# The first loads on two queues: x rows 2 and 3 issued by ScalarE, wq unbroken on SyncE, q products by token halves

## The chip, the cores and the metric

The kernel runs on one core of a Trainium2 chip, with bfloat16 inputs and output. The metric is device time in microseconds (us). Engines are named as in the profile: PE (TensorE matmul), PEld (its weight loads), DVE (VectorE), ACT (ScalarE), POOL (GpSimd), SP (SyncE, which here only issues DMAs). "SPq" and "ACTq" rows are DMA issues of those two engines.

## The reference

One token batch of 2048 x 512 goes through two branches that a sigmoid gate mixes: an attention with a compressive memory over four segments of 512 tokens (32 heads of 16), and a ReGLU feed-forward with 1792 hidden units.

```
g = sigmoid((x * gate_w).sum(-1, keepdims=True))
q, k, v = x @ wq, x @ wk, x @ wv                 # 32 heads of 16, 4 segments of 512 tokens
for s in range(4):
    p = softmax(qs @ ks.T * 16**-0.5 + mask)     # causal inside the segment
    a_mem = (phi(qs) @ M) / (phi(qs) @ z + 1e-6) # phi(t) = t + 1 if t > 0 else exp(t)
    outs.append(sigmoid(beta) * a_mem + (1 - sigmoid(beta)) * (p @ vs))
    M, z = M + phi(ks).T @ vs, z + phi(ks).sum(0)
a = concat(outs) @ wo
b = (relu(x @ W_gate) * (x @ W_up)) @ W_down
out = g * a + (1 - g) * b
```

## The kernel before, in words

The program is planned in Python while it is built. `program` makes a list of operations (`Op`), each with its engine or engines, what it reads and writes, and an assumed duration; they stand in queues, one for each kind of work, and each queue has one letter. The string `ORDER` (line 24) says which queue gives its next operation, letter by letter; `Sched.place` appends it to its engine's instruction list and adds the semaphore waits that its inputs need. So the order on every engine is written out by hand, as one long string, and `BANKS` (line 37) names the PSUM bank that each accumulation takes. Each engine then runs its own list strictly in order.

PSUM is split in two: `psL`, four banks that hold one block of attention logits at a time, and `psA`, four banks that all other accumulations share. A bank of `psA` can be written again only after DVE or ACT has copied it out.

The work of a segment, as PE sees it:

- L540 / L549 / L547: the products of q, k (channels on the partitions) and v (tokens on the partitions). Segment 0's q products (L540) are made of 256 tokens each, 32 in all: four groups of 128 channels, four rows of wq (`wq0` to `wq3`, 128 input channels each) and two halves of tokens.
- L650: attention logits, one block of 512 columns on four row groups of the array ("quad"), which ACT turns into exponentials (L654, tile `E`) and POOL masks (L659); L682: the products of E with v (`vaug` and a shifted copy `vsh`); L592 and L612: the memory.
- L742: gate and up products of the feed-forward, which ACT or DVE turn into `rl` (L750, L751) and DVE into `hT` (L753); L781 and L774: the down and output products, evacuated at L790 and L791 and stored at L793.

What stands around the change is the start. Segment 0's x is loaded as four row blocks of 128 tokens into `hT` (called x rows 0 to 3 here, 128 KB each), transposed on PE against the identity (L448, 16 products, one for each row block and 128 channels), copied out of psL into `xT` by DVE (L453) and ACT (L455), first for rows 0 and 1 (256 tokens, "half 0"), then for rows 2 and 3 ("half 1"). Five products of constants (L439) and two more (L461) run on PE before there is data. All the loads of the start are issued by SP through `load` (line 355, DMA at L356): x rows 0 and 1, `wq0`, x rows 2 and 3, `wq1` to `wq3`, then wk, wv, half of wg and of wu, two small constants (`braw`, `gwb`), the other halves, and the transposing loads of the next segment's x. Each uses one of 16 semaphores in turn. Three tiny loads of 1 KB (`touch`) are issued by ACT. `gwb` is needed by the gate sums (L491) that DVE makes of the four x rows.

```
    load_x0(0)
    load_x0(1)
    load_w("wq", V.wq, A_wq, (0,))
    load_x0(2)
    load_x0(3)
    load_w("wq", V.wq, A_wq, (1, 2, 3))
```

Of the kernel before, what the change touches and what calls it, by code (L numbers as in the profile page):

```python
# [7 lines left out]
ACT = mybir.ActivationFunctionType  # L8
# [3 lines left out]
F32 = mybir.dt.float32  # L12
# [307 lines left out]
def program(sc, nc, T, PL, PA, A_x, A_wq, A_wk, A_wv, A_wo, A_beta, W_g, W_u, W_d, gate_w, out, NSEG, KT, NF, NT, EPS, SCALE):  # L320
    V = type("V", (), T)

    def op(eng, fn, occ, **k):
        return sc.add(Op([(eng, fn, occ)], **k))

    def pe(fn, occ, **k):
        k.setdefault("lat", PE_LAT)
        if k.get("role") == "w":
            k["reads"] = list(k.get("reads", ())) + [f"init{i}" for i in range(4)]
        return op("pe", fn, occ, **k)  # L330

    def dve(fn, occ, **k):
        return op("dve", fn, occ, **k)
# [4 lines left out]
    def act(fn, occ, **k):  # L338
        return op("act", fn, occ, **k)
# [4 lines left out]
    def dma(eng, fn, nbytes, occ=500.0, **k):  # L344
        return op(eng, fn, occ, dma=True, nbytes=nbytes, **k)

    def A(ep):
        return PA[:, ep.bank, :] if ep.nb == 1 else PA[:, ep.bank:ep.bank + 2, :]

    def xt(c):  # L350
        return [f"xT{c}_{kt}" for kt in range(KT)] if c else [f"xT0_{kt}{h}" for kt in range(KT) for h in range(2)]

    lact, lsp = [], []

    def load(eng, names, dst, src, nbytes, occ=460.0):
        (lact if eng == "act" else lsp).append(dma(eng, lambda e, dst=dst, src=src: e.dma_start(dst, src), nbytes, occ=occ, writes=names, name="ld" + names[0]))  # L356
# [36 lines left out]
    lact = []  # L393
# [42 lines left out]
    def warm(m, n, k, b):  # L436
        def fn(e):
            for i in range(m):
                ins = e.matmul(PL[:, b, 0:n], lhsT=nc.const_aps.tensor(1.0, [128, 128], BF16), rhs=nc.const_aps.tensor(1.0, [128, n], BF16), start=True, stop=True)  # L439
            return ins  # L440
        return pe(fn, m * n * (0.834 if k == 0 else 0.5), writes=[f"bankL{b}"], name=f"warm{k}")

    xps, xcs = [warm(5, 512, 0, 3)], []
    for h in range(2):
        for i in (2 * h, 2 * h + 1):
            for kt in range(KT):
                def fx(e, i=i, kt=kt):
                    return e.matmul(PL[:, kt, 128 * (i % 2):128 * (i % 2) + 128], lhsT=V.hT[:, i, kt * 128:(kt + 1) * 128], rhs=V.ident[:], start=True, stop=True)  # L448
                xps.append(pe(fx, 60 if h else 85, reads=[f"hT{i}", "ident"], writes=[f"bankL{kt}"], name=f"xt{i}_{kt}"))
        for kt in range(KT):  # L450
            src, dst = PL[:, kt, 0:256], V.xT[:, kt, 256 * h:256 * h + 256]
            if kt % 2 == 0:
                xcs.append(dve(lambda e, d=dst, x=src: e.tensor_copy(d, x), t_dve(256), reads=[f"bankL{kt}"], writes=[f"xT0_{kt}{h}"], name=f"xc{kt}{h}"))  # L453
            else:
                xcs.append(act(lambda e, d=dst, x=src: e.activation(d, x, ACT.Copy), t_act(256), reads=[f"bankL{kt}"], writes=[f"xT0_{kt}{h}"], name=f"xc{kt}{h}"))  # L455
# [75 lines left out]
    def proj(s):  # L531
# [3 lines left out]
        def pj(w, col, name, wname, tokmajor=False):  # L535
            ep = epq3 if s == 0 and name == "q" and col == 3 else Epoch()
            if s == 0 and name == "q":
                for k0, h in ((0, 0), (1, 0), (0, 1), (1, 1), (2, 0), (3, 0), (2, 1), (3, 1)):
                    def fh(e, k0=k0, h=h):
                        return e.matmul(A(ep)[:, 256 * h:256 * h + 256], lhsT=w[:, k0, col * 128:(col + 1) * 128], rhs=V.xT[:, k0, tok + 256 * h:tok + 256 * h + 256], start=(k0 == 0 and h == 0), stop=(k0 == KT - 1 and h == 1))  # L540
                    pes.append(pe(fh, mm(256), reads=[f"{wname}{k0}", f"xT0_{k0}{h}"], name=f"{name}{s}_{col}", ep=ep, role="w2" if ep is epq3 or pes and pes[-1].ep is ep else "w"))
                return ep
            for k0 in range(0, KT, 2):
                def fn(e, k0=k0):
                    for kt in range(k0, k0 + 2):
                        if tokmajor:
                            ins = e.matmul(A(ep)[:, :], lhsT=V.xT[:, kt, tok + col * 128:tok + (col + 1) * 128], rhs=w[:, kt, :], start=(kt == 0), stop=(kt == KT - 1))  # L547
                        else:
                            ins = e.matmul(A(ep)[:, :], lhsT=w[:, kt, col * 128:(col + 1) * 128], rhs=V.xT[:, kt, tok:tok + 512], start=(kt == 0), stop=(kt == KT - 1))  # L549
# [343 lines left out]
```

## Time and profile before

| | us |
|---|---|
| median of 3 runs | 265.36 (265.15 to 265.53) |
| the profiled execution | 264.96 |
| its span on the core | 262.9 |
| PE busy | 258.9 |
| ACT busy | 189.5 |
| DVE busy | 183.9 |
| POOL busy | 124.2 |

The span is counted from the first to the last instruction of the program. A timeline row reads: start, duration (us), engine, line, operation, out<-in, number of instructions, and in brackets the idle time of the engine before it with what ended it. Matmul ends are modelled, and successive matmuls overlap: the rate at which PE works is read from the distance of two starts.

### The profile page before, as it was taken

What the parts mean: (1) busy time and instruction counts of PE and PEld (TensorE: products, weight loads), DVE (VectorE), ACT (ScalarE), POOL (GpSimd) and SP (SyncE); (2) the same over time, 40 slices, a digit from 0 to 9 for tenths busy, and PEclk for the clock granted to TensorE, in tenths of its full rate; (3) what the DMA queues carried; (4) which work ended last, traced back from release to release, by engine and by line L of the source; (5) the groups of instructions that cost most, each with busy time, mean ns of one, the idle gap of its engine ahead of it and who ended that gap; (6) DMA issues with size and microseconds to landing.
All of it is one profiled execution on the core that took longest, in us unless ns stands there. A gap on an engine that the chain in (4) does not pass through costs nothing.

```text
span 262.9 us, 6634 instructions
## 1 busy us (share of the span) xinstructions
PE 258.9 (98%) x2761; PEld 115.2 (44%) x2761; DVE 183.9 (70%) x360; ACT 189.5 (72%) x167; POOL 124.2 (47%) x283
## 2 busy tenths in 40 slices
PE   7999999999999999999999999999999999999996
PEld 4644344434344444434434444444444444444444
DVE  5689898878884398887874678967871726569800
ACT  3588898889897787887786797577885767765021
POOL 3038364754546437845454455644653446334000
PEclk9999999999999999999999999999999999999999
DMA  5989535374041222333220230010231000010011
GB/s 178 265 301 268 116 63 144 57 244 86 18 107 42 63 62 41 62 82 60 53 61 16 61 82 22 20 25 3 42 85 37 5 20 22 20 22 0 2 40 42
DMA packets 34686, 19.36 MB, mean 74 GB/s; under 512 B 24033, under 2 KB 34145, under 8 KB 34657
## 3 DMA queue, kind: packets, MB, share of 16 engines
q1 hardware_dynamic: 34560, 18.93, 29.0%
q8 instruction: 22, 0.36, 0.6%
q14 instruction: 8, 0.06, 0.1%
q10 hardware_dynamic: 96, 0.00, 0.0%
HBM read 9.87 MB, written 2.11 MB: 46 GB/s over the span
## 4 chain that ended last, share of the span: by engine, by line
PE 97%; DMA 1%; SPq 1%; issue 0%; DVE 0%
PE psA L742 39%; PE psA L781 19%; PE psA L549 9%; PE psL L650 9%; PE psA L682 7%; PE psA L547 6%; PE psA L774 5%; PE psA L612 1%; PE psA L540 1%; DMA wq<-in_A_wq_dram 1%; SPq L356 1%; PE psA L592 1%; DVE osb L790 0%; PE psL L448 0%
## 5 line engine op out<-in xcount | busy, mean ns | idle before, releaser
L659 POOL TENSOR_SCALAR_AFFINE_SELECT E<-E 64x256 bf16<-64x256 bf16 (+1 forms) x256 | 115.4, 461 | 114.3 <-ACT E L654 106.0
L654 ACT ACTIVATE E<-psL 128x2048 bf16<-128x2048 f32 x72 | 135.1, 1876 | 30.2 <-PE psL L650 28.0
L742 PE MATMUL psA<-xT,wu 128*128 128x512 bf16 x224 | 61.8, 380 | 0.0
L742 PE MATMUL psA<-xT,wg 128*128 128x512 bf16 x224 | 61.0, 380 | 0.0
L781 PE MATMUL psA<-wd,hT 128*128 128x512 bf16 (+2 forms) x238 | 58.2, 367 | 0.0
L753 DVE TENSOR_TENSOR hT<-psA,rl 128x512 bf16<-128x512 f32 x56 | 38.3, 684 | 15.8 <-PE psA L742 14.2
L750 ACT ACTIVATE rl<-psA 128x512 bf16<-128x512 f32 x36 | 21.3, 596 | 16.4 <-PE psA L742 16.4
L781 PEld LDWEIGHTS psA<-wd,hT 128*128 128x128 bf16 x238 | 21.6, 98 | 24.6 <-issue 2.4
L742 PEld LDWEIGHTS psA<-xT,wu 128*128 128x128 bf16 x224 | 20.2, 98 | 25.3 <-issue 3.2
L742 PEld LDWEIGHTS psA<-xT,wg 128*128 128x128 bf16 x224 | 19.9, 98 | 25.2 <-issue 3.9
L650 PE MATMUL psL<-qT,kp 32*128 32x192 bf16 (+7 forms) x512 | 28.8, 287 | 0.1
L692 DVE STREAM_TRANSPOSE Tn<-psA 128x512 f32<-128x512 f32 x32 | 21.1, 695 | 9.0 <-PE psA L682 8.8
L650 PEld LDWEIGHTS psL<-qT,kp 32*128 32x128 bf16 x512 | 8.3, 92 | 26.7 <-issue 11.0
L682 PE MATMUL psA<-E,vaug 64*17 64x128 bf16 (+7 forms) x512 | 18.7, 283 | 0.0
L682 PE MATMUL psA<-E,vsh 64*17 64x128 bf16 (+7 forms) x512 | 18.3, 283 | 0.0
L547 PE MATMUL psA<-wv,xT 128*128 128x512 bf16 x64 | 17.7, 380 | 0.0
L751 DVE TENSOR_SCALAR rl<-psA 128x512 bf16<-128x512 f32 x20 | 13.8, 690 | 4.5 <-PE psA L742 4.2
L790 DVE TENSOR_SCALAR osb<-psA,omg 128x512 bf16<-128x512 f32 (+1 forms) x7 | 4.8, 687 | 17.0 <-PE psA L774 11.0
L549 PE MATMUL psA<-xT,wk 128*128 128x512 bf16 x64 | 16.6, 380 | 0.0
L774 PE MATMUL psA<-wo,oT 128*128 128x512 bf16 (+2 forms) x68 | 16.5, 367 | 0.0
L791 ACT ACTIVATE osb<-psA,omg 128x512 bf16<-128x512 f32 (+1 forms) x10 | 6.8, 676 | 13.0 <-PE psA L774 10.6
L682 PEld LDWEIGHTS psA<-E,vaug 64*17 64x17 bf16 x512 | 11.6, 86 | 7.4 <-issue 3.6
(72 smaller groups left out, 234.7 us busy)
## 6 DMA issues: line engine op xcount, KB each, us to landing
vsh<-vaug SPq DMA_DIRECT2D x8, 272.0 KB, 3.6
out_dram<-osb SPq DMA_DIRECT2D x15, 128.0 KB, 1.7
wg<-in_B_W_gate_dram SPq DMA_DIRECT2D x8, 224.0 KB, 5.6
wu<-in_B_W_up_dram SPq DMA_DIRECT2D x8, 224.0 KB, 5.3
osb<-in_A_x_dram SPq DMA_DIRECT2D x12, 128.0 KB, 2.3
wd<-in_B_W_down_dram SPq DMA_DIRECT2D x3, 512.0 KB, 4.5
hT<-in_A_x_dram SPq DMA_DIRECT2D x4, 128.0 KB, 2.2
wq<-in_A_wq_dram SPq DMA_DIRECT2D x4, 128.0 KB, 2.8
```

The lines of the kernel that those rows point to most:

```text
L547: ins = e.matmul(A(ep)[:, :], lhsT=V.xT[:, kt, tok + col * 128:tok + (col + 1) * 128], rhs=w[:, kt, :], start=(kt == 0), stop=(kt == KT - 1))
L549: ins = e.matmul(A(ep)[:, :], lhsT=w[:, kt, col * 128:(col + 1) * 128], rhs=V.xT[:, kt, tok:tok + 512], start=(kt == 0), stop=(kt == KT - 1))
L650: ins = q.matmul(PL[:, jj, o:o + 512 - 64 * c], lhsT=V.kp[r, kslot(s, G), c, :], rhs=V.qT[r, qslot(s, G), 64 * c:512], start=True, stop=Tr ...
L654: acts.append(act(lambda a: a.activation(V.E[:, e, :, :], PL[:, :, :], ACT.Exp, scale=SCALE), t_act(2048), reads=[f"bankL{b}" for b in ran ...
L659: pools.append(pool(lambda g, ap=ap, base=base: g.affine_select(out=ap, in_=ap, compare_op=ALU.is_ge, fill=0.0, base=base, pattern=[[0, 4] ...
L682: ins = q.matmul(A(eps[p])[32 * jj:32 * jj + 17, 64 * c:512], lhsT=v[:, 8 * G + 2 * jj + p, :], rhs=V.E[r, e, jj, o:o + 512 - 64 * c], sta ...
L692: ds.append(dve(lambda e, p=p, ep=eps[p]: e.transpose(V.Tn[:, p, :], A(ep)[:, :]), 706, writes=[f"Tn{p}"], name=f"tr{s}_{G}_{p}", ep=eps[p ...
L742: ins = e.matmul(A(ep)[:, :], lhsT=w[:, kt, f * 128:(f + 1) * 128], rhs=V.xT[:, kt, c * 512:(c + 1) * 512], start=(kt == 0), stop=(kt == K ...
L750: evs.append(sc.add(Op([("act", lambda e, ep=eg, r=r: e.activation(V.rl[:, r, :], A(ep)[:, :], ACT.Relu), t_act(512)), ("dve", lambda e, e ...
L753: evs.append(dve(lambda e, ep=eu, r=r, hs=hs: e.tensor_tensor(V.hT[:, hs, :], A(ep)[:, :], V.rl[:, r, :], ALU.mult), t_dve(512), reads=[f" ...
L774: ins = e.matmul(A(ep)[:, 0:c1 - c0], lhsT=V.oT[:, o0 + G, i * 128:(i + 1) * 128], rhs=V.wo[:, G, c0:c1], start=st_ and G == 0, stop=sp_ a ...
L781: ins = e.matmul(A(ep)[:, 0:c1 - c0], lhsT=V.hT[:, slots[f], i * 128:(i + 1) * 128], rhs=V.wd[:, f, c0:c1], start=st_ and f == f0, stop=sp ...
```

## The change

x rows 2 and 3 are issued by ACT, behind an exponential of one column that writes a scratch tile, instead of by SP behind `wq0`. SP issues x rows 0 and 1, then all of wq, then goes on as before. Segment 0's q products are put in another order: all four rows of wq with half 0 of the tokens for the four groups (16 products), then group by group the same with half 1 (16 products). The planner is told other sizes for the loads and a due time for the transposes of rows 2 and 3, and the strings `ORDER` and `BANKS` are written anew as a whole, which moves operations on all engines and in all segments.

```diff
 ORDER = (
-    "gefafafefafefafefaefaggfgagggggahgihaisggsagggsggashsigssahsisssasbsssassssassssCassssBsasssCsasBasbasDsasaHEsHasyIaDpasaIwsIasDsaFsysSaIpsFaSwuIauFsa"
...
+    "hafgbgbgfgbgfgbgafgbafgbhhghbhhhhhihbjijbtttbttttbthhhhbthtithjbhttitjtbtttctbttttDbttttCtbtttDtbtCbtbtFtbctIbItFbtbFJqbJtzJJtbEtxbtSvGbttJbHJtSvzbtG"
...
 BANKS = (
-    "012312301230123012301231023012301320312013201320123013201321302310321032031201202012230130120120120130231203120302323013201320132102002302012013013013"
...
+    "012312301230120320321031203213021302130213021302130213012301230123012031031201220203010132302302303210321302013203232013201320312303202030130123123120"
...
-    def load_x0(i):
-        load("sp", [f"hT{i}"], V.hT[:, i, :], x0[:, i, :], 150000)
+    def load_x0(i, eng="sp"):
+        load(eng, [f"hT{i}"], V.hT[:, i, :], x0[:, i, :], 140000)
...
-            load("sp", [f"{nm}{kt}"], w[:, kt, :], src[kt * 128:(kt + 1) * 128, :], 410000 if (nm, kt) == ("wk", 0) else 160000)
+            load("sp", [f"{nm}{kt}"], w[:, kt, :], src[kt * 128:(kt + 1) * 128, :], 360000 if (nm, kt) == ("wk", 0) else 140000)
     load_x0(0)
     load_x0(1)
-    load_w("wq", V.wq, A_wq, (0,))
-    load_x0(2)
-    load_x0(3)
-    load_w("wq", V.wq, A_wq, (1, 2, 3))
+    load_w("wq", V.wq, A_wq, range(KT))
+    lact.append(act(lambda e: e.activation(V.rden[:, 0:1], nc.const_aps.tensor(1.0, [128, 1], F32), ACT.Exp), 1500, writes=["rden"], name="tab"))
+    load_x0(2, "act")
+    load_x0(3, "act")
+    sc.queue(0, lact)
     load_w("wk", V.wk, A_wk, range(KT))
...
+                if h:
+                    xps[-1].after = 5400.0
...
-                for k0, h in ((0, 0), (1, 0), (0, 1), (1, 1), (2, 0), (3, 0), (2, 1), (3, 1)):
+                for k0, h in ((0, 0), (1, 0), (2, 0), (3, 0), (0, 1), (1, 1), (2, 1), (3, 1)):
```

The sizes given to `load` and the time `after` only steer the planner's bookkeeping; the data moved is the same.

The order at the start of PE before (L439 and L461 are the products of constants, L448 the transposes of x, L540 the q products, L549 the k products):

```order
1 L439 MATMUL psL<-const-bfloat16-1.0 128x512 x5
2 L448 MATMUL psL<-ident,hT 128x128 x8
3 L461 MATMUL psA<-const-bfloat16-1.0 128x256 x2
4 L540 MATMUL psA<-xT,wq 128x256
5 L448 MATMUL psL<-ident,hT 128x128 x2
6 L540 MATMUL psA<-xT,wq 128x256
7 L448 MATMUL psL<-ident,hT 128x128 x3
8 L540 MATMUL psA<-xT,wq 128x256
9 L448 MATMUL psL<-ident,hT 128x128 x2
10 L540 MATMUL psA<-xT,wq 128x256 x2
11 L448 MATMUL psL<-ident,hT 128x128
12 L540 MATMUL psA<-xT,wq 128x256 x27
```

And of the change (lines are three further down; L653 is a block of logits, L550 the v products, L745 the gate and up products):

```order
4 L543 MATMUL psA<-xT,wq 128x256 x8
5 L449 MATMUL psL<-ident,hT 128x128 x5
6 L543 MATMUL psA<-xT,wq 128x256
7 L449 MATMUL psL<-ident,hT 128x128
8 L543 MATMUL psA<-xT,wq 128x256 x2
9 L449 MATMUL psL<-ident,hT 128x128 x2
10 L543 MATMUL psA<-xT,wq 128x256 x21
11 L552 MATMUL psA<-xT,wk 128x512 x14
12 L653 MATMUL psL<-qT,kp 128x512 x4
13 L552 MATMUL psA<-xT,wk 128x512 x2
14 L550 MATMUL psA<-wv,xT 128x512 x6
15 L745 MATMUL psA<-xT,wg 128x512 x2
```

Eight q products now stand ahead of the first transpose of x row 2, where one stood; the fifth transpose of the half is the first that needs x row 3. The last row of wq is first needed by the 13th q product, and 20 q products remain from there.

ACT at the start of the change, whose first rows before were the table load, the four copies into xT and the first tiny load:

```order
1 L369 ACT_TABLE_LOAD
2 L369 ACTIVATE rden<-const-float32-1.0 128x1
3 L356 DMA hT<-in_A_x_dram 128x512 x2
4 L458 ACTIVATE xT<-psL 128x256 x4
5 L356 DMA adT<-in_B_W_gate_dram 16x32
```

The table load belongs to the new exponential; the two x loads follow it.

DVE of the change, from the copy of k's last group to the first gate sums (L494, which need gwb) and the `hT` product after them:

```order
6 L565 CAST kT<-psA 128x512
7 L531 TENSOR_SCALAR ttmp<-kT 128x1024
8 L578 CAST vaug<-psA 128x32x16
9 L569 TENSOR_SCALAR kp<-kT,pm 128x8x64 x2
10 L532 TENSOR_TENSOR ek<-ek,ttmp 128x1024
11 L578 CAST vaug<-psA 128x32x16
12 L754 TENSOR_SCALAR rl<-psA 128x512
13 L531 TENSOR_SCALAR ttmp<-kT 128x1024
14 L756 TENSOR_TENSOR hT<-psA,rl 128x512
15 L494 ISA hT,gl<-hT,gwb 128x512
...
17 L494 ISA hT,gl<-hT,gwb 128x512
...
19 L756 TENSOR_TENSOR hT<-psA,rl 128x512
```

Before, all four v copies of this segment, the small constants made from `braw` and the first `hT` product stood ahead of the first gate sum; now two v copies and that `hT` product do, and the second `hT` product, which frees the bank of the second up accumulation, waits behind two gate sums.

More of the change, by code (lines that the diff above doesn't have):

```diff
@@ new lines @@
+    "eTAvTtJtMeDTqtTJxvETvTvAvMzTqdArMTvxAvprQMUUyAqTtUAtxTtATdtUGtTtHATqSvHvAxVRtMTtTvAvVHqRtLATvxdTtJvCTtTtJtFMTqTtoxvdvCTptTMtTqTSFrxSvATVvvAzTvMqTVtTLA"
+    "vTRxttAdCvvAtMTqFvToxtvMTptTtJtDJvATFqTvMxTvTtMrozqTpAvTWxvAvWMttAHtTAvHAvLqTAsTxvPTouuMunTnpPqTuoxPTuTuXuuTqOuTJxYJupTsuTPuPuPTqTuXTxsTuPtPuPtTOXqTGu"
+    "xYsuPuPuyTPqTupTxRuXvrSTSyquATxvTAuTvMTvuNKTTAKYvTRvuALRvqMTvxvovMpurMTqVTQvxAuvSrVAUUMTquUAxTuATuUtBvoquxATpvSvtMTVvTHNqTvxTMVvTvJvJMTvYTqovxvMTpvTve"
+    "MTvTAvLvMeTqTArxeMTvAvevTALqTvAxTvTMvvAvoLvAvnMTnpqTLvAxvosTMtTtPvBDvPTAqTLvpTPxvTvBtMvtTLtETtrKJCqRWtxAvWAttEtTqADtTAxvAvtMTtTEtTqADTtTxtBvETXvtMtTqH"
@@ L36 @@
+    "wwwwwOwwwwwYNY"
 )
 BANKS = (
-    "012312301230123012301231023012301320312013201320123013201321302310321032031201202012230130120120120130231203120302323013201320132102002302012013013013"
-    "21020230232013201320132013201320201313210310210210210231023102312312312320"
+    "012312301230120320321031203213021302130213021302130213012301230123012031031201220203010132302302303210321302013203232013201320312303202030130123123120"
+    "32020230120123012301230213021301312012032321020201201201230120312031203120"
```

16 lines of the change are left out of this document (6 added, 10 removed).

## The prediction

> **What bounds the kernel now.** I read the page first (the span and PE's share), then the chain of waits, then the list of waits with PE alone, then the timeline of PE and of SP over the first 10 us.
>
> ```profile
> span 262.9 us, 6634 instructions
> PE 258.9 (98%) x2761; PEld 115.2 (44%) x2761; DVE 183.9 (70%) x360; ACT 189.5 (72%) x167; POOL 124.2 (47%) x283
> PE psL L439 <- PEq L878: 0.8, 1, 0.8
> PE psA L540 <- DMA wq<-in_A_wq_dram: 0.5, 1, 0.5
> PE psA L540 <- DVE xT L453: 0.2, 1, 0.2
> ```
>
> The last three rows are the whole list of PE's waits: who waited for whom, total, times, longest. PE waits for the program's start, and twice during the first q products; after those it never waits again in 250 us. So PE's own work sets the end, and an edit can move it in three ways only: PE starts its unbroken run earlier, its run gets longer, or a wait appears in it.
>
> The work in the run is the same after the change. The two orders hold the same products, and PE goes over between the full array (q, k, v, feed-forward, output) and the tiled products (logits, E with v, memory) 164 times in both, so that the price of going over cancels too. The last rows are also alike: the same wo and wd products of the last three token blocks in the same order. What is left is the start and new waits.
>
> The start on PE:
>
> ```profile
> 2.93 1.06 PE L448 MATMUL psL<-ident,hT 128*128 128x128 bf16 x8
> 4.50 0.27 PE L540 MATMUL psA<-xT,wq 128*128 128x256 bf16 x1 [0.20 <-DVE xT L453]
> 5.00 0.33 PE L448 MATMUL psL<-ident,hT 128*128 128x128 bf16 x3
> 6.14 0.28 PE L540 MATMUL psA<-xT,wq 128*128 128x256 bf16 x1 [0.49 <-DMA wq<-in_A_wq_dram]
> 6.26 0.22 PE L448 MATMUL psL<-ident,hT 128*128 128x128 bf16 x1
> 6.32 3.11 PE L540 MATMUL psA<-xT,wq 128*128 128x256 bf16 x27
> 9.27 3.19 PE L549 MATMUL psA<-xT,wk 128*128 128x512 bf16 x14
> ```
>
> Between the first q product at 4.50 and the first k product at 9.27 lie 32 q products and eight transposes. A q product takes (3.11 - 0.27) / 26 = 0.109 us from start to start, a transpose (0.33 - 0.22) / 2 = 0.055. That is 3.49 + 0.44 = 3.93 us of work in 4.77; the other 0.84 is lost, most of it before `wq1` landed. I call the start of the k products T; it is 9.27 now, and from there 253 us of work follow without a wait.
>
> **The change part by part.** I work T out as the latest of four bounds.
>
> PE's own work: the first q product still waits for `wq0` and the first copy, so T cannot be below 4.50 + 3.93 = **8.43**.
>
> The loads on SP:
>
> ```profile
> 2.19 0.91 SPq L356 DMA_DIRECT2D hT<-in_A_x_dram  x2
> 3.14 1.38 SPq L356 DMA_DIRECT2D wq<-in_A_wq_dram  x3
> 3.14 2.96 DMA wq<-in_A_wq_dram
> wq<-in_A_wq_dram SPq DMA_DIRECT2D x1, 128.0 KB, 2.8
> hT<-in_A_x_dram SPq DMA_DIRECT2D x1, 128.0 KB, 2.4
> 4.56 1.85 SPq L356 DMA_DIRECT2D wk<-in_A_wk_dram  x4
> wk<-in_A_wk_dram SPq DMA_DIRECT2D x1, 128.0 KB, 3.2
> ```
>
> The third row is from the chain: `wq1` is issued at 3.14 and lands 2.96 later, at 6.10; PE goes on at 6.14. The rows with one DMA and a last number are its time from issue to landing, for `wq3` (issued at 3.14 + 1.38 - 0.43 = 4.09, landed at 6.89), for x row 3 (2.67, 5.07) and for `wk3` (5.98, 9.2). SP issues every (1.38 - 0.43) / 2 = 0.475 us.
>
> `wq3` now stands where `wq1` stood, sixth on SP, and is issued at 3.14. Its landing lies between 6.10, if ACT's two loads take nothing from it, and 6.89, if the eight loads of x and wq land no faster together than the eight before. The DMA engines' share decides between the two:
>
> ```profile
> 3.00:4.00 1.00, 1.00 (x11) 0.93 (x9) 0.45 (x3) 0.19 (x1) 0.05 (x1) 1.00 0.80 241
> 5.00:6.00 1.00, 0.66 (x9) 0.42 (x6) 0.64 (x2) 0.38 (x1) 0.00 (x0) 1.00 0.84 226
> 8.00:9.00 1.00, 1.00 (x12) 0.90 (x10) 0.41 (x1) 0.60 (x1) 0.00 (x0) 1.00 0.98 303
> ```
>
> (The last two columns are the busy share and GB/s.) At 3 to 6 us they were 80 to 84% busy, with 226 to 241 GB/s; at 8 us 98% and 303. So a second issuer finds room for about a fifth more, and I take 6.4, nearer to the lower end. From `wq3` on, 20 q products remain, 4 of half 0 and 16 of half 1: T = landing + 0.04 + 20 x 0.109 = landing + 2.22, which is **8.62** (8.32 to 9.11).
>
> A rule of the Trainium skill speaks against this step: "DMA: Bandwidth & Descriptors", section "Issuing engines are not separate DMA queues", says that DMAs from several engines share the same 16 DMA engines, and that issuing from more than one saves only the issuing time. The busy share of 0.80 in the row above agrees that there was issuing time to save, and the 0.98 that there is little more; taken strictly the rule gives the upper end, and that case is the first rival below.
>
> x row 3 on ACT:
>
> ```profile
> 0.80 1.28 ACT L455 ACT_TABLE_LOAD   x1 [0.80 <-PEq L878]
> 6.52 0.38 ACT L455 ACTIVATE xT<-psL 128x256 bf16<-128x256 f32 x1 [0.61 <-PE psL L448]
> 6.53 0.38 ACTq L356 DMA_DIRECT2D adT<-in_B_W_gate_dram  x1
> 3.71 0.76 DVE L453 CAST xT<-psL 128x256 bf16<-128x256 f32 x2 [0.55 <-PE psL L448]
> adT<-in_B_W_gate_dram ACTq DMA_DIRECT2D x1, 1.0 KB, 3.0
> adT<-in_B_W_up_dram ACTq DMA_DIRECT2D x1, 1.0 KB, 3.8
> adT<-in_B_W_down_dram ACTq DMA_DIRECT2D x1, 1.0 KB, 5.9
> ```
>
> ACT's DMA of 6.53 is issued as soon as the activation ahead of it has begun, so the two x loads leave when the exponential begins, at 0.80 + 1.28 = 2.08, and about 0.43 later, at 2.5: 0.1 to 0.2 before SP issued them. If ACT lets them pass the waiting exponential they leave at 0.8 and 1.2 and land earlier; x rows 0 and 1 then share the DMA engines with them, which moves 4.50 rather than the end of the list. With the 2.4 of x row 3 the landing is at 4.9, with the 3.0 of ACT's first load at 5.5. After it come 0.04, four transposes (0.22), 0.26 from a transpose to its copy (6.26 to 6.52), two copies (0.76) and 14 products (1.53): T = landing + 2.81, so 7.7 to 8.3. It does not bind. The exponential costs nothing: ACT had the table load at that time anyway and nothing to do until 3.81.
>
> wk: SP issues it two places, 0.95 us, earlier. The second pair of k products needs `wk3` at T + 0.43; at the worst it lands at 9.2 as now, which gives T = 8.81, with its latency kept at 8.25 and T = 7.9. Below the 8.62 for all but the worst part.
>
> Sum: T = 8.62 instead of 9.27, **0.65 us less**, bounds 0.16 and 0.84.
>
> New waits in the rewritten order can take some of it back. The densest place that I find is the DVE list of the first segment, where two gate sums, which need gwb, now stand ahead of the second `hT` product:
>
> ```profile
> 12.73 0.43 SPq L356 DMA_DIRECT2D gwb<-in_gate_w_dram  x1
> gwb<-in_gate_w_dram SPq DMA_DIRECT2D x1, 128.0 KB, 6.3
> L753 DVE TENSOR_TENSOR hT<-psA,rl 128x512 bf16<-128x512 f32 x5 | 3.4, 688 | 0.7 <-ACT rl L750 0.5 <-PE psA L742 0.2
> L529 DVE TENSOR_TENSOR ek<-ek,ttmp 128x1024 bf16<-128x1024 bf16 x2 | 1.7, 826 | 0.0
> L566 DVE TENSOR_SCALAR kp<-kT,pm 128x512 bf16<-128x512 bf16 x8 | 2.8, 367 | 0.2
> L528 DVE TENSOR_SCALAR ttmp<-kT 128x1024 bf16<-128x1024 bf16 x2 | 1.3, 642 | 0.0
> 20.59 1.18 DVE L491 CUSTOM_DVE_ANT_0 hT<-hT,gwb 128x512 bf16<-128x512 bf16 x1
> 22.51 0.68 DVE L753 TENSOR_TENSOR hT<-psA,rl 128x512 bf16<-128x512 f32 x1
> 13.36 0.69 DVE L562 CAST kT<-psA 128x512 bf16<-128x512 f32 x1
> 18.00 0.40 PE L650 MATMUL psL<-qT,kp 32*128 32x256 bf16 x8
> 18.33 0.60 PE L547 MATMUL psA<-wv,xT 128*128 128x512 bf16 x2
> ```
>
> DVE copies k's last group at T + 4.09 (13.36 now). With that copy, ten steps lead to the first gate sum: five of 0.69 (copies, relu, `hT`), two of 0.64, two of 0.37, one of 0.83, in all 6.3 us, so T + 10.4, which is 19.0. gwb lands at 12.73 + 6.3 = 19.0 now, and not later after the change. Two gate sums take 22.51 - 20.59 = 1.92, `hT` 0.69: the bank is free at T + 13.0. PE asks for it (by `BANKS`) with the fourth gate accumulation, after 56 products of (3.19 - 0.38) / 13 = 0.216 and three blocks of logits that each add 0.33 + 0.1: T + 13.4. It is covered with 0.4 to spare; if gwb came at 19.4 the cover would be gone, and each later us costs PE one. For the rest of the order I take no wait, since the list above shows none in 250 us of the order before; the bounds of that are 0 and, if one such place in each segment fell short by its 0.4, 1.6.
>
> The profiled execution took 264.96, 2.06 more than its span, and 0.40 less than the median of 265.36. 264.96 - 0.65 = 264.31 on its scale, **264.7** as a median.
>
> **The rivals.** *The transfers were the bound all along.* All eight loads land as before, `wq3` at 6.89, T = 9.11: 265.2, no change. For it: landings already trailed issues by more and more (2.4 for x row 3, 2.8 for `wq3`, 3.2 for `wk3`). Against it: the busy share of 0.80. *Slower: x row 3 comes late from ACT's queue*, and PE stands before its transposes with eight q products done and all else behind them. ACT's own small loads took 3.0, 3.8 and 5.9. It decides from a landing at 9.27 - 2.81 = 6.46 on, a latency of 4.0; with 5.9 it lands at 8.4, T = 11.2, and the median is 267.3; with 4.6 at 7.1, 266.0. Against it: the 5.9 was met at 15.9 us with the DMA engines full. *The new order gives it back*: the gate sums meet a gwb at 19.9, or another bank is short, 0.5 us in all: 265.2. *The change does not do what it says*: ACT issues the x loads only after the exponential has ended and its queue has started up, say 0.4 later, 5.9 for x row 3, T = 8.7: 264.8, hardly told from the forecast.
>
> **How the numbers follow.** About 0.2% of the median, 0.53 us, is what a measurement of this kernel can tell from no change. The forecast has 0.50, the transfers as the bound 0.25, the late x row 0.10, the new waits 0.15. Faster by over 0.53 needs a median below 264.83, T below 8.74 without new waits: most of the first case, 0.45. Slower takes the late x row and the worse part of the new waits: 0.19. The rest, 0.36, lies within. The range reaches from 264.3 (T at its lowest, 264.5, and a measurement's 0.2) to 266.0.
>
> **What would show it.** T, the first k product's start, at 8.4 to 8.8 and PE's waits below 0.5 us between the first q product and T; a landing of `wq3` near 6.4 and of x row 3 before 5.8; no PE wait after T. I am wrong if T is above 9.0, or if the list of PE's waits has new rows after T that sum to more than 0.3 us.

## The result, and the profile after

The change makes the kernel slower: 265.86 us median of 22 runs against 264.93 us median of 22 runs of the kernel before on the same chip, ratio 1.0053 with a 95% interval of 1.0033 to 1.0073 (the ratio is of means without one run of 331.03; the medians alone give 1.0035). The forecast was 264.7. The runs of the change stand in two groups: 13 at 265.26 to 266.05 and 8 at 267.14 to 268.51; those of the kernel before make one group, 264.01 to 265.93. The profiled run of the change took 267.23 and belongs to the upper group; its span is 265.3, 2.4 more than before.

The page, and the whole list of PE's waits:

```profile
span 265.3 us, 6637 instructions
PE 260.9 (98%) x2761; PEld 116.1 (44%) x2761; DVE 186.6 (70%) x364; ACT 185.9 (70%) x164; POOL 123.1 (46%) x283
PE psL L440 <- PEq L881: 0.8, 1, 0.8
PE psL L653 <- issue: 0.7, 1, 0.7
PE psA L543 <- DMA wq<-in_A_wq_dram: 0.3, 1, 0.3
```

PE sets the end as before, with as many products and 2.0 us more of busy time: it worked more slowly somewhere. One wait is new, and no engine and no DMA is named as its releaser: "issue".

The timeline of ACT, SP and PE at the start:

```profile
0.80 1.28 ACT L369 ACT_TABLE_LOAD   x1 [0.80 <-PEq L881]
0.86 0.87 ACTq L356 DMA_DIRECT2D hT<-in_A_x_dram  x2
2.10 0.20 ACT L369 ACTIVATE rden<-const-float32-1.0 128x1 f32<-128x1 f32 x1
1.73 3.40 DMA wq<-in_A_wq_dram
3.19 1.30 PE L449 MATMUL psL<-ident,hT 128*128 128x128 bf16 x8
5.27 1.86 PE L543 MATMUL psA<-xT,wq 128*128 128x256 bf16 x8 [0.34 <-DMA wq<-in_A_wq_dram]
6.93 0.74 PE L449 MATMUL psL<-ident,hT 128*128 128x128 bf16 x5
8.42 2.76 PE L543 MATMUL psA<-xT,wq 128*128 128x256 bf16 x21
11.01 1.24 PE L552 MATMUL psA<-xT,wk 128*128 128x512 bf16 x5
```

Three things are to be seen. ACT issues its two x loads at 0.86, while the table load runs and before the exponential at 2.10: they pass it. They then share the DMA engines with x rows 0 and 1 and `wq0`, which lands at 1.73 + 3.40 = 5.13 instead of 4.37, and the first q product starts at 5.27 instead of 4.50. And the eight q products from 5.27 to 6.93 are (6.93 - 5.27) / 8 = 0.21 us apart, twice the 0.109 of the kernel before. T is 11.01, not 8.62.

The new wait, in PE's timeline:

```profile
46.37 0.66 PE L595 MATMUL psA<-vaug,phik 128*32 128x34 bf16 x64
46.96 1.04 PE L745 MATMUL psA<-xT,wg 128*128 128x512 bf16 x4
49.03 0.39 PE L653 MATMUL psL<-qT,kp 32*128 32x256 bf16 x6
50.09 0.28 PE L653 MATMUL psL<-qT,kp 32*128 32x256 bf16 x2 [0.67 <-issue]
```

It falls inside a block of logits, after six of its eight products. The program places its waits for semaphores only ahead of a block, so no semaphore can be the cause: the last two starts at the wait are 0.94 us apart. The kernel before has the same break, unnoticed because the list of waits doesn't show it, inside its block at 47.16, where two starts are 0.40 apart (that block takes 0.80 instead of 0.40):

```profile
44.23 1.90 PE L547 MATMUL psA<-wv,xT 128*128 128x512 bf16 x8
47.16 0.80 PE L650 MATMUL psL<-qT,kp 32*128 32x256 bf16 x8
```

The 2.42 us by which PE ends later in the profiled run are then T with 1.74, this break with 0.54, and 0.13 at the third block of logits (22.5 us), which waits for an exponential that ACT began 1.2 us late. ACT was late because each of its three 1 KB loads into `adT` waits until the one before has landed; they now start at 8.67 instead of 6.53 and meet full DMA engines, and the exponential of 20.53 stands behind the third:

```profile
8.67 0.34 ACTq L356 DMA_DIRECT2D adT<-in_B_W_gate_dram  x1
13.31 0.37 ACTq L356 DMA_DIRECT2D adT<-in_B_W_up_dram  x1
20.17 0.32 ACTq L356 DMA_DIRECT2D adT<-in_B_W_down_dram  x1
20.53 1.88 ACT L657 ACTIVATE E<-psL 128x2048 bf16<-128x2048 f32 x1 [1.58 <-PE psA L745]
```

### The profile page after: what moved, and what is told of

It is laid out like the page before. It is cut to its first block, busy times and chain, and to the rows that moved or that the text cites. A ratio compares the mean times of both kernels' runs of the same rounds, so it can differ in the third digit from the quotient of the medians.

```text
span 265.3 us, 6637 instructions
## 1 busy us (share of the span) xinstructions
PE 260.9 (98%) x2761; PEld 116.1 (44%) x2761; DVE 186.6 (70%) x364; ACT 185.9 (70%) x164; POOL 123.1 (46%) x283
## 4 chain that ended last, share of the span: by engine, by line
PE 92%; DMA 6%; ACT 1%; issue 0%; SPq 0%; DVE 0%; ACTq 0%
PE psA L745 36%; PE psA L784 19%; PE psL L653 9%; PE psA L552 8%; PE psA L685 7%; PE psA L777 5%; PE psA L550 4%; DMA adT<-in_B_W_up_dram 3%; DMA adT<-in_B_W_gate_dram 2%; DMA wq<-in_A_wq_dram 1%; PE psA L615 1%; PE psA L543 1%; ACT E L657 1%; PE psA L595 1%; PE psL L449 0%
## 5 line engine op out<-in xcount | busy, mean ns | idle before, releaser
L745 PE MATMUL psA<-xT,wg 128*128 128x512 bf16 x224 | 60.9, 380 | 0.0
L745 PE MATMUL psA<-xT,wu 128*128 128x512 bf16 x224 | 60.5, 380 | 0.0
L784 PE MATMUL psA<-wd,hT 128*128 128x512 bf16 (+2 forms) x238 | 57.1, 367 | 0.0
L784 PEld LDWEIGHTS psA<-wd,hT 128*128 128x128 bf16 x238 | 20.9, 98 | 24.2 <-issue 4.3
L745 PEld LDWEIGHTS psA<-xT,wu 128*128 128x128 bf16 x224 | 20.2, 98 | 25.6 <-issue 2.8
L745 PEld LDWEIGHTS psA<-xT,wg 128*128 128x128 bf16 x224 | 20.4, 98 | 25.2 <-issue 2.4
L653 PE MATMUL psL<-qT,kp 32*128 32x192 bf16 (+7 forms) x512 | 28.8, 287 | 0.7 <-issue 0.7
L754 DVE TENSOR_SCALAR rl<-psA 128x512 bf16<-128x512 f32 x28 | 19.2, 687 | 10.3 <-PE psA L745 10.1
L753 ACT ACTIVATE rl<-psA 128x512 bf16<-128x512 f32 x28 | 16.7, 596 | 12.2 <-PE psA L745 12.2
L653 PEld LDWEIGHTS psL<-qT,kp 32*128 32x128 bf16 x512 | 8.3, 92 | 26.6 <-issue 11.5
L552 PE MATMUL psA<-xT,wk 128*128 128x512 bf16 x64 | 17.3, 380 | 0.0
L550 PE MATMUL psA<-wv,xT 128*128 128x512 bf16 x64 | 16.9, 379 | 0.0
L793 DVE TENSOR_SCALAR osb<-psA,omg 128x512 bf16<-128x512 f32 (+1 forms) x10 | 7.1, 706 | 12.7 <-PE psA L777 11.7
L794 ACT ACTIVATE osb<-psA,omg 128x512 bf16<-128x512 f32 (+1 forms) x7 | 4.7, 671 | 14.6 <-PE psA L777 14.0
```

Of the source, the lines that this page charges most:

```text
L653: ins = q.matmul(PL[:, jj, o:o + 512 - 64 * c], lhsT=V.kp[r, kslot(s, G), c, :], rhs=V.qT[r, qslot(s, G), 64 * c:512], start=True, stop=Tr ...
L745: ins = e.matmul(A(ep)[:, :], lhsT=w[:, kt, f * 128:(f + 1) * 128], rhs=V.xT[:, kt, c * 512:(c + 1) * 512], start=(kt == 0), stop=(kt == K ...
L754: ("dve", lambda e, ep=eg, r=r: e.tensor_scalar(V.rl[:, r, :], A(ep)[:, :], 0.0, None, ALU.max), t_dve(512))],
L784: ins = e.matmul(A(ep)[:, 0:c1 - c0], lhsT=V.hT[:, slots[f], i * 128:(i + 1) * 128], rhs=V.wd[:, f, c0:c1], start=st_ and f == f0, stop=sp ...
```

## The experiments

The theories, as they stood after the two traces. **Clock**: PE starts at half rate and reaches its full one only after some time of work without a break; the later x row 1 and `wq0` make breaks. **Order**: the rewritten lists bring their own waits, whatever the loads do; later this became **fetch**: PE's instructions come by DMA in pieces, and PE runs out of them. **Transfers**: the loads alone decide. Each comparison is with runs of the kernel before on the same chip in the same batch; the ratio compares means, the first two columns are medians.

| run | median us | before | ratio, 95% interval | runs above 266 |
|---|---|---|---|---|
| e1 start filled | 266.09 | 264.74 | 1.0034 to 1.0079 | 7 of 11 |
| e2 loads put back | 266.67 | 264.74 | 1.0049 to 1.0095 | 9 of 11 |
| e3 loads held | 265.73 | 264.74 | 1.0026 to 1.0070 | 3 of 12 |
| e4 loads alone | 264.70 | 264.74 | 0.9985 to 1.0027 | 3 of 12 |
| e5 list shifted 37 | 264.64 | 264.65 | 0.9993 to 1.0032 | 2 of 12 |
| e6 before, shifted 35 | 264.87 | 264.65 | 1.0000 to 1.0033 | 1 of 12 |
| e7 shifted 65 | 265.57 | 264.65 | 1.0018 to 1.0047 | 2 of 12 |
| e8 three repairs | 264.37 | 264.65 | 0.9975 to 0.9996 | 0 of 12 |
| e9 shifted 80 | 265.82 | 265.08 | 1.0013 to 1.0043 | 3 of 12 |
| e10 shift, 1 KB loads freed | 264.54 | 265.08 | 0.9983 to 1.0031 | 4 of 12 |
| e11 shift, start filled | 264.90 | 265.08 | 0.9980 to 1.0005 | 0 of 12 |
| e12 repairs, old order | 265.04 | 265.08 | 0.9985 to 1.0022 | 2 of 12 |
| e13 wd behind | 265.44 | 264.85 | 1.0009 to 1.0054 | 5 of 12 |
| e14 before, wd ahead | 267.53 | 264.85 | 1.0077 to 1.0126 | 6 of 6 |
| e15 wo and wd behind | 265.08 | 264.85 | 1.0007 to 1.0054 | 5 of 12 |
| e16 the change again | 266.10 | 264.85 | 1.0034 to 1.0077 | 7 of 12 |

**Loads or order?** e1 to e4 take the change apart.

e1 gives PE work in the breaks:

```diff
+    def warm_m(e):   # placed behind the transposes of x row 0
+        for _ in range(2):
+            ins = e.matmul(PL[:, 3, 256:512], lhsT=<ones 128x128>, rhs=<ones 128x256>, start=True, stop=True)
...
     def warm1(e):
-        for _ in range(2):
+        for _ in range(4):
```

> The change with PE's idle time at the start filled: two more products of constants (128x256) between the transposes of x row 0 and those of x row 1, and four instead of two ahead of the first q product. Clock theory (PE works at half rate until it has been busy without a break for some us, and the breaks that the later x row 1 and wq0 make put this off in some runs): no run above 266.5, q products 0.109 us apart soon after the first one, T 9.2 to 9.5, time 265.3 to 265.8. Rival (the slow q products have nothing to do with PE's breaks): 3 to 4 runs in 10 stay at 267 to 268.5 as with the change.

e2 has the loads of before with the order of the change:

```diff
-    load_w("wq", V.wq, A_wq, range(KT))
+    load_w("wq", V.wq, A_wq, (0,))
+    load_x0(2)
+    load_x0(3)
+    load_w("wq", V.wq, A_wq, (1, 2, 3))
...
-    load_x0(2, "act")
-    load_x0(3, "act")
```

> The change with its loads put back: x rows 2 and 3 on SP behind wq0, the exponential kept, the new order of all operations kept. Clock theory: first q product at 4.5, T about 9.1 (wq3 at 6.9 + 2.2), one group of times and none above 266.5. Order theory (the rewritten order costs 0.135 us at the fourth block of logits and 0.54 us near 50 us whatever the loads do): both waits are still there, time 265.2 to 265.6. If all of the loss came from the loads: 264.5 to 264.9.

e3 makes ACT's loads wait for the exponential's result:

```diff
     def load_x0(i, eng="sp"):
-        load(eng, [f"hT{i}"], V.hT[:, i, :], x0[:, i, :], 140000)
+        load(eng, [f"hT{i}"], V.hT[:, i, :], x0[:, i, :], 140000, reads=["rden"] if eng == "act" else ())
```

> The change with ACT's two x loads made to wait for the result of the exponential, so that they leave at about 2.4 and 2.8 as the prediction assumed. Clock theory and the prediction's sum: x rows 0 and 1 land at 2.85 and 3.23, wq0 at 4.4, the first q product starts at 4.5, q products 0.109 apart, T 8.5 to 8.9, no run above 266.5; time 264.4 if the new order costs nothing, 264.9 to 265.2 if its two waits (0.135 and 0.54) remain. Rival (wq3 is bound by the transfers whichever engine issues): T 9.1, 265.4 with the waits.

e4 is the kernel before with the lines of the change on the loads (the exponential, x rows 2 and 3 on ACT, all of wq on SP) and its own order otherwise:

> The kernel before with the loads of the change alone (exponential and x rows 2 and 3 on ACT, wq unbroken on SP), its own order of everything else. Clock theory: the first q product starts near 5.3, T is 9.2 to 9.4 in most runs and about 11 in 3 to 4 runs in 10, so times of 264.9 to 265.2 and 266.5 to 267. Order theory: the waits at 22.5 and 50.1 us are absent. If the loads are harmless: one group, 264.5 to 265.

e4 against the others answers it: the loads alone cost nothing in the median (264.70 against 264.74; three of 12 runs are above 266, where the 33 of the kernel before have none), while all three kernels with the new order lose 1.0 to 1.9 us, e2 with the loads of before among them. e1 and e2 missed: neither has a single group, and e2 should have come out at 265.6 at most. Their profiles say why. The break that I had taken for a fixed 0.54 isn't fixed:

```profile
PE psL L660 <- issue: 2.5, 1, 2.5
PE psL L654 <- issue: 1.7, 1, 1.7
PE psL L653 <- issue: 1.3, 1, 1.3
```

These are PE's waits inside the same block of logits in e1, e2 and e3. Against the 0.40 of before, the distance of the two starts grew to 2.75, 1.95 and 1.56.

On the loads e3 shows the rest. With the hold, x rows 0 and 1 and `wq0` land at 2.83, 3.23 and 3.95, and the first q product starts at 4.21; but q products stay 0.21 apart, and transposes 0.107, until 6.35, so T is 9.24 (worked out from the last q product, since that trace lacks the first k product). e2 is alike, at half rate until 6.6.

**Instructions as data.** The page counts the DMAs that bring instructions:

```profile
q8 instruction: 22, 0.36, 0.6%
```

They are 16 KB each. PE's list has 2761 products, each with its weight load, and some 50 separate waits, about 5570 instructions. 0.36 MB over these is 64 bytes each, so q8 fits PE's list, and a piece holds 256 instructions; in e5, whose list stands 37 products later, the third of these DMAs starts at 40.36 instead of 47.77. Counted in the traces, the break stands in both kernels ahead of the same place, about the 960th instruction, though other work stands there. In every profile that has the break, PE goes on 2.3 to 2.9 us after the third of these DMAs has started (before: 45.36 to 47.67; the change: 47.77 to 50.09; e1: 47.42 to 50.02). Fitted over the complete traces, a DMA mostly starts some 1 to 3 us after PE has come within about 300 instructions of the border. Ahead of this border those 150 products are 64 products of the memory (0.66 us), 64 of E with v (1.1 us), two blocks of logits and a few large ones, 4.3 us in all before and 4.4 in the change; every other border of the two has 7.9 us or more.

e5 moves the border off that stretch, by small products of constants in place of the large ones at the start, for as long:

```diff
-    xps, xcs = [warm(5, 512, 0, 3)], []
+    xps, xcs = [warm(42, 64, 0, 3)], []
```

> The change with the five products of constants at the start (128x512) replaced by 42 small ones (128x64) that should fill the same 2.3 us. Nothing else differs, but each product stands 37 places later in PE's list of instructions. Fetch theory (PE runs out of fetched instructions at the 467th product, because the 121 products before it, small ones of the memory and of E with v, take only 2.7 us, less than a fetch needs): by the profile of the change the shortest such stretch is then 5.0 us, so the wait inside the block of logits near 50 us is gone and no other takes its place; most runs at 264.5 to 265.0, some above 266 left from the half rate of the start. Rival (the wait belongs to that place in the program: a semaphore, a bank, E with v): it is still there, 265.5.

e6 does it in the kernel before (`warm(40, 68, 0, 3)`), e7 and e9 shift the change further, to where I reckoned another dense stretch (60 of 128x45 and 12 of 128x44 for `warm1`; 70 of 128x39 and 17 of 128x30):

> The kernel before with 40 small products of constants (128x68) in place of its five large ones, so that its list stands 35 places later. Fetch theory: the stretch of 121 products that took 3.8 us and cost a wait of 0.37 at 47.7 us gives way to a shortest one of 5.1; the wait goes and the time falls by 0.3 to 0.5, to 264.2 to 264.5. Rival: no difference, 264.7.

> The change with its list put 65 places later instead of 37 (60 products of 128x45 at the start and 12 of 128x44 in place of the later two). Fetch theory: the wait near 50 us is gone here too, but a stretch of 121 products that takes only 1.6 us (from 161.0 to 162.7 in the profile of the change) now stands just where a fetch is due, so PE waits 1.5 to 4 us in a block of logits near 162.7 us; time 266.5 to 269. Rival (shifting the list only removes a wait at one place, or does nothing): 264.6 to 265.5.

> The change with its list put 80 places later (70 products of 128x39 at the start, 17 of 128x30 in place of the later two). Fetch theory with exact counts: PE's waits so far came each time ahead of the 962nd instruction of its list (two for a product, one for a separate wait) in the kernels of both orders, and a new piece of 256 instructions begins every 256 from there; the shift by 65 put such a border behind a stretch of 140 products that took 5.1 us, which was enough; the shift by 80 puts it behind one that takes 2.5 us (160.5 to 163.0 in the profile of the change). So PE waits 1 to 3 us for an issue between 162 and 164 us, the wait near 50 us is gone, and the time is 265.8 to 268. Rival (fetches are late only early in the program, or with other loads running): no wait there, 264.5 to 265.5.

e5 is the clean hit: 264.64 against 264.65 for the kernel before, where the unshifted change is 0.93 to 1.25 above it, and nothing differs after the start but 37 places in the list. No PE wait over 0.2 is left after T in its profile (the 0.2s there are single products that the trace lacks), the one at the third block neither. In e6 the break is gone too, but the time did not fall as expected; its profile shows another stretch that broke:

```profile
20.04 0.23 ACT L468 ACTIVATE eb<-braw 128x32 f32<-128x32 bf16 x1 [2.38 <-DMA braw<-in_A_beta_dram]
PE psL L650 <- ACT E L654: 1.1, 1, 1.1
```

`braw` landed at 20.0 instead of 17.35, ACT stood before it, and PE behind ACT. e7 and e9 missed: no wait came at 162 us. In e9 the DMA had started at 157.8 with 287 instructions to go, 3.5 us ahead of the border: the stretch before it was longer than I had counted, since I let the DMA be due 280 instructions ahead and it is due earlier, at about 300; with that it is 4.7 us. In e9's profile PE waits 1.0 us for the late `eb` constant at 28 us instead. What else costs e7 and e9 their 0.7 to 0.9 isn't settled.

**The sum without the losses.** e8 is e3 and e5 together, with the 1 KB loads under names of their own, so that none waits for another:

```diff
     def touch(n, src):
-        load("act", ["adT"], V.adT[0:16, 32 * n:32 * n + 32], src, 1024)
+        load("act", [f"tch{n}"], V.adT[0:16, 32 * n:32 * n + 32], src, 1024)
```

> The change with three repairs: ACT's two x loads wait for the exponential, the list is shifted by 37 places with 42 small products, and the three 1 KB loads on ACT no longer wait for one another. Theory (loads, fetch and those waits together were the whole loss): first q product at 4.2 to 4.5, no PE wait after T over 0.2, T between 8.5 and 9.5 depending on when PE comes to its full rate; 263.9 to 264.6, below before. Rival (half rate at the start takes all that the loads could win, whatever is repaired): 264.6 to 265.2.

e10 is e5 with the freed 1 KB loads, e11 is e5 with the filled start of e1, e12 is the kernel before with e8's three repairs:

> The run with the list shifted by 37 places, with the three 1 KB loads on ACT freed from one another and nothing else. If those waits cost (0.135 us at the fourth block of logits in the profile of the change), the median is 264.4 to 264.6; if they are covered, as with the shift alone, 264.6 to 264.7. The x loads still pass the exponential, so 1 to 3 runs in 12 above 266 remain, and the distance from here to the run with all three repairs (264.37, none above 264.9) is what the real wait for the exponential brings.

> The shift by 37 places and the filled start together (38 products of 128x70, two of 128x256 between x rows 0 and 1, four ahead of the first q product). Clock theory (the runs above 266 of the shift alone come from breaks in PE's work, which put off its full rate): none above 265.8, median 264.5 to 264.9. Rival (those runs have another cause): 1 to 3 of 12 above 266.

> The kernel before, its own order of everything but the start's loads, with the three repairs of the fastest run so far: x rows 2 and 3 on ACT behind a real wait, the list 35 places later (no stretch of 140 products under 7 us at a border), the 1 KB loads freed. If the rewritten order itself is worth nothing once fetches are out of the way: 264.2 to 264.5, as there. If the new order of the q products is worth something: 264.6 to 265.0. If this order keeps the late small constant that cost 1.1 us in the shifted kernel before: a group at 265.5.

e8 is faster than the kernel before, 264.37 against 264.65, the interval just below 1, all runs within 263.87 to 264.86. Its start:

```profile
4.30 0.61 PE L543 MATMUL psA<-xT,wq 128*128 128x256 bf16 x4
5.34 0.61 PE L543 MATMUL psA<-xT,wq 128*128 128x256 bf16 x4 [0.43 <-DMA wq<-in_A_wq_dram]
6.71 2.46 PE L543 MATMUL psA<-xT,wq 128*128 128x256 bf16 x21
```

The products are 0.109 apart from the start, and T is 6.71 + 21 x 0.1095 = 9.01: even here `wq1`, landed at 5.29, holds PE for 0.43 after four products, and x row 3, landed at 6.10, once more. e10 against e5 tells nothing of the 1 KB loads, since its runs again stand in two groups, 264.25 to 264.57 and five from 265.71 on. That grouping is the test of the clock theory, with the break out of the way: with ACT's loads let pass and the start unfilled 2 of 12 (e5) and 4 of 12 (e10) are above 266; with the start filled (e11) or the loads held (e8) none of 24 is. That is 6 of 24 against none; that half rate is behind those six is argued from the one profile of the upper group, the change's at 267.23, since no run above 266 of e5 or e10 was profiled. In e12, two of whose runs are above 266, held loads did harm: its order wants x row 2 after the first q product, it landed at 6.12, and PE stood for 1.4 us.

```profile
6.17 0.29 PE L449 MATMUL psL<-ident,hT 128*128 128x128 bf16 x2 [1.41 <-DMA hT<-in_A_x_dram]
```

**Why the fetch is later in the change.** Both orders have the dense stretch; the change loses more there. SP's list differs: the change puts the first 512 KB load of wd ahead of two transposing loads, right behind wo and an x row.

```profile
42.22 0.58 SPq L356 DMA_DIRECT2D wo<-in_A_wo_dram  x1
42.84 0.51 SPq L499 DMA_DIRECT2D osb<-in_A_x_dram  x1
43.39 0.43 SPq L356 DMA_DIRECT2D wd<-in_B_W_down_dram  x1
45.00:46.00 1.00, 1.00 (x6) 0.29 (x3) 1.00 (x4) 1.00 (x2) 0.16 (x1) 1.00 1.07 376
46.00:47.00 1.00, 1.00 (x74) 0.72 (x74) 1.00 (x3) 1.00 (x2) 0.66 (x2) 1.00 1.08 384
45.00:46.00 1.00, 1.00 (x6) 0.29 (x3) 1.00 (x2) 1.00 (x1) 0.85 (x2) 1.00 0.39 127
```

The first two windows are of the change; their last columns, share and GB/s, show full DMA engines until 47 us. The last row is the kernel before, where the share falls to 0.39 at 45 to 46, when its fetch starts. e13 moves wd back behind the two transposing loads, e15 moves wo too, e14 moves wd ahead in the kernel before; only letters of SP's queue in `ORDER` change places. e16 is the change itself.

> The change with one DMA moved in SP's list: the first 512 KB load of wd, which the new order puts ahead of two transposing loads of ek, goes back behind them, where the kernel before has it. PE's list isn't shifted. Theory (PE's fetch of instructions, due near 45 us, stands behind the 512 KB loads of wo and wd on the DMA engines; with both in front of it, it starts at 46.2 to 47.8 and PE waits 0.9 to 2.7): the fetch starts earlier, the wait in the block of logits near 50 us falls to 0.5 or less, median 264.9 to 265.3. Rival (the dense run of small products alone makes the fetch late, whatever is loaded): the wait stays at 0.9 to 2.7, time as with the change.

> The kernel before with the same DMA moved the other way: the first load of wd right behind wo and the x row, ahead of the two transposing loads. Theory: the fetch of 45.4 us comes 0.5 to 2 us later and the wait of 0.4 us at 47.3 grows to 0.9 to 2.5; median 0.4 to 1.5 above before, with nothing else changed. Rival: no difference beyond 0.2.

> The change with both large loads, wo and the first of wd, behind the two transposing loads. Theory: the DMA engines are free when the fetch is due, it starts 0.9 to 1.5 us after PE passes the 304th instruction ahead of the border, as at the other borders, and PE waits less than 0.2; median 264.5 to 264.9, as with the shifted list, with the few runs above 266 that the start makes. Rival: as the change.

> The change itself, once more beside the others on the same chip. Theory: q products at half rate for between 1 and 4 us after the first one, T between 9.2 and 11, a PE wait of 0.5 to 2.7 near 50 us whose end stands 2.3 to 2.6 after the start of a fetch; median 265.5 to 266.2.

e14 is the sharpest run of the study: one DMA moved ahead makes the kernel before 2.7 us slower. Its profile, PE first and then windows of one us:

```profile
46.73 0.39 PE L650 MATMUL psL<-qT,kp 32*128 32x256 bf16 x5
48.78 0.29 PE L650 MATMUL psL<-qT,kp 32*128 32x256 bf16 x3 [1.66 <-issue]
47.00:48.00 1.00, 0.11 (x5) 0.00 (x0) 1.00 (x2) 0.27 (x1) 1.00 (x4) 1.00 0.00 0
49.00:50.00 1.00, 1.00 (x8) 0.51 (x6) 0.00 (x0) 0.89 (x1) 0.00 (x0) 0.95 0.53 106
50.00:51.00 1.00, 1.00 (x4) 0.30 (x2) 0.00 (x0) 0.98 (x1) 0.00 (x0) 0.50 0.39 59
51.00:52.00 1.00, 1.00 (x4) 0.34 (x3) 0.22 (x1) 0.00 (x0) 0.88 (x3) 0.50 0.92 264
52.00:53.00 1.00, 1.00 (x4) 0.42 (x3) 1.00 (x3) 0.00 (x0) 0.71 (x2) 0.50 0.69 242
```

The fetch started at 46.30, 0.9 later than before though PE came to the border 0.4 sooner, and the wait grew to 1.66. What follows is a second loss: the granted clock (third column from the right) falls to 0.50 for 3.4 us, which costs some 1.6 us more. Its mean over the run, 0.994, marks such runs: four of e14's six have it, and elsewhere it stands only at the slowest runs of kernels with the break (268.51 of the change, 268.79 of e1, 268.47 and 269.94 of e2, 268.75 of e3, 268.29 of e16). No run of a shifted kernel has it. Nor does each break bring it: after the longer wait of 2.5 in e1's profile the granted clock stays at 1.00.

e13 met the expected break, 0.3 us at most in its profile (264.63 us), but not the median: five of its runs are above 266, which fits the unfilled start, though none of the five was profiled. e15 missed: with both loads gone the DMA engines moved nothing from 43 to 45 us, and yet the fetch started 2.3 us after it was due, not 0.9 to 1.5, and PE waited:

```profile
43.00:44.00 1.00, 1.00 (x6) 0.29 (x3) 1.00 (x4) 1.00 (x2) 0.17 (x1) 1.00 0.00 0
44.00:45.00 1.00, 1.00 (x74) 0.74 (x74) 1.00 (x3) 1.00 (x2) 0.65 (x2) 1.00 0.00 0
PE psL L653 <- issue: 0.5, 1, 0.5
```

So the dense stretch alone cost up to 0.72 by the distance of the two starts, and with both large loads in front of the fetch it was 0.94 to 2.75. What sets the 1 to 3 us from due to start, 2.3 in e15 with the DMA engines idle, stays open. e16 shows the break at 1.4 us and T at 9.71 with products at full rate, waiting 1.0 us for `wq0`.

## Why the prediction was wrong

*What bounds the kernel* was right: PE's busy time sets the end, no step of ACT, DVE or POOL took its place. But "an edit can move it in three ways only" left out a fourth: PE's own rate. And the list of waits, from which I read that PE "never waits again in 250 us", hid a wait of 0.4 in the kernel before that sat inside a busy group.

*PE's own work, T not below 8.43.* This step failed. It priced 32 q products at 0.109 and eight transposes at 0.055, and held that 4.50 would stay. The rate held in the kernel before because its PE waited for `wq1` until 6.14 anyway, so that any half rate up to there cost nothing; once wq comes unbroken, the rate is what T hangs on. Measured: first q product at 5.27, products 0.21 apart to 9.05, T = 11.01 in one run, 9.71 at full rate in another. A page of the Trainium skill has the rule, and the prediction left it out: "TensorE: Matmul & The Clock Gate", section "Part 1: The HAM clock gate", says that PE works at half its clock until it has been busy for a window of about 3.4 us that runs free of the kernel's start, so that the point varies from run to run. By it, as an estimate, an unbroken start at 0.84 would come to full rate between 4.2 and 7.6; the traces agree (at or before 4.8 in the kernel before, 6.35 in e3, 6.6 in e2), and the one profile of the upper group, with breaks in its start, has it at 9.05. Breaks don't always put it off: e16's start has longer ones, and its first q products, from 5.77, are 0.109 apart.

*x row 3 on ACT, "the two x loads leave when the exponential begins".* Wrong, and the sentence behind it had the truth: they left at 0.86 and 1.28 and moved the first q product from 4.50 to 5.27. The prediction named this and then gave it neither a place in the sum nor a rival. The row of 6.53 was read too widely: the activation ahead of that DMA waited for PE, and the exponential waits for nothing. That x row 3 doesn't bind came true by luck: it landed at 4.43 because it left early. Held as the prediction assumed, it landed at 5.84 in e3 and at 6.10 in e8, after the 4.9 to 5.5 expected; with the prediction's own 2.81 that gives T = 8.65 and 8.91, above its 8.62.

*The loads on SP.* `wq3` at 6.4 was nearly right: 6.55, between the two bounds (6.78 in e3 and 6.47 in e8, where the x loads leave as assumed). What SP's later loads gained, the first ones lost: x row 1 came 0.6 and `wq0` 0.8 later. e4 puts the sum of it at zero, as the rival of the transfers had it, for another reason.

*New waits.* The DVE place did hold, and gwb landed at 18.77. "For the rest of the order I take no wait" failed twice: 0.13 on ACT's chain of 1 KB loads, and the fetch with 0.54 in one profile, 1.3 in the other and up to 2.35 in kernels that share the order. The upper bound given, 1.6, was of the right size, but its mechanism was a bank; the rival that the new order gives it back had 0.15 and should have led. e5 shows that this term carries the loss of the lower group: without it the median is that of the kernel before.

*The sum* of 0.65 less was not met by any version; e8, with everything repaired, comes to T = 9.01, because `wq1` at 5.29 holds the fifth q product, a bound that the four of the prediction lacked.

## What to carry

In this kernel, with one engine 98% busy, three supplies still set the time, and the list of waits shows them in part or not at all: the rate at which the engine works, the instructions, and the first operands. When the whole order is rewritten, look for the densest run of small products and for large loads issued just ahead of it, and compare distances of starts, not the listed waits. When a load is moved to an idle queue to come earlier, ask what it now shares the DMA engines with: the load that PE needs first should have them alone.

## What the hardware showed

- A DMA on ACT's queue passed an activation that stood ahead of it and had nothing to wait for: issued at 0.86 during a table load from 0.80 to 2.08, ahead of the activation at 2.10. Behind an activation that waited for PE it left only as that one began, though they share no tile: 6.53 behind 6.52 in the kernel before, 8.67 behind 8.66 in the change.
- PE's instructions came in pieces of 256 by DMA, most of them within 0.9 to 1.4 us; PE went on 2.3 to 2.9 us after the start of one, and a stretch of 150 products in 4.3 us outran it by 0.26 to 2.75 in every profile of a list that wasn't shifted; one in 4.7 (e9) did not.
- A wait of 1.66 us was followed by 3.4 us at a granted clock of 0.50. The profile shows that spell, yet it gives 1.00 for the start, where q products 0.21 apart were at half rate as well:

```profile
5.00:7.00 2.00, 1.73 (x9) 1.24 (x10) 0.00 (x0) 0.00 (x0) 0.00 (x0) 1.00 0.88 262
```
